# Zero products for an idle TensorE, and a longer reckoned way from a matmul to its reader, in a scheduled attention and GLU block

## The chip, the cores and the metric

The kernel runs on one core of one Trainium2 chip. The metric is device time in microseconds (us), lower is better. A run here is one execution; every comparison is made between runs of the changed program and runs of the kernel before on the same chip in the same rounds. Ratios are the mean time of one kernel's fast runs over that of the other's of the same rounds, so they are not quite the ratio of the medians that are quoted.

The engines: TensorE (PE; its weight loads are PEld), VectorE (DVE), ScalarE (ACT), GpSimd (POOL), SyncE (SP, which here only issues DMAs).

## The reference, cut to what matters

```python
x = A_x                                                   # 1 x 2048 x 640, bf16
h  = x + attention(layernorm(x), A_wqkv) @ A_wo           # 32 heads of 20
h2 = h + ((n @ w_gate) * (n @ w_up)) @ w_down             # n = layernorm(h), F = 1728
```

Attention has 32 heads x 2048 x 2048 scores. Their exponentials are the bulk of ACT's work; a part of them is made on DVE by a bit trick. The score products use 20 rows of the array, four heads side by side in four row groups; the products with the values fill 32 columns, four heads side by side in four column groups.

Of the kernel before, what the change touches and what calls it, by code (L numbers as in the profile page):

```python
# [17 lines left out]
P = 128  # L18
# [39 lines left out]


LAT = 0.12  # L60
DMA_LAT = 1.5
SWITCH = 0.105


def c_act(n):
# [78 lines left out]
def kernel(  # L144
# [30 lines left out]
    R = sb.tile([P, RW], BF16, name="R")  # L175
    WO = sb.tile([P, KT, D], BF16, name="WO")
    IDN = sb.tile([P, P], BF16, name="IDN")
    NEA, NEB, NY = 5, 4, 28
    EA = [sb.tile([P, 1536], BF16, name=f"EA{i}") for i in range(NEA)]
    EB = [sb.tile([P, 1024], BF16, name=f"EB{i}") for i in range(NEB)]  # L180
# [53 lines left out]
            heapq.heappush(coming[e], (op.avail, seq[0], op))  # L234
        tick(op.avail)

    def finish(op, t):
        op.done = t
        for u in op.users:
            u.left -= 1  # L240
            u.avail = max(u.avail, t)
            if u.left == 0:
                if isinstance(u, Op):
                    enqueue(u)
                else:
                    release_later(u.avail, u.cb)
        op.users = []
        tick(t)
# [31 lines left out]
    def try_start(e):  # L280
        t = now[0]
        if free[e] > t + 1e-9:
            return False
        c = coming[e]
        while c and c[0][0] <= t + 1e-9:
            _, s_, op = heapq.heappop(c)
            heapq.heappush(ready[e], (op.key, s_, op))
        held = []
        got = None
        while ready[e]:  # L290
            item = heapq.heappop(ready[e])
            op = item[2]
            if op.done is not None:
                continue
            if op.gate is not None and not op.gate():
                held.append(item)
                continue
            other = "POOL" if e == "DVE" else "DVE"
            if op.lock and e in lockt and lockt[other] > t + 1e-9:
                held.append(item)  # L300
                tick(lockt[other])
                continue
            got = op
            break
        for h_ in held:
            heapq.heappush(ready[e], h_)
        if got is None:
            return False
        end = t + (got.dur[e] if isinstance(got.dur, dict) else got.dur)
        free[e] = end  # L310
        if got.lock and e in lockt:
            lockt[e] = end
        if got.hook is not None:
            got.hook(t, end, e)
        got.fn(e)
        finish(got, end + got.lat)
        tick(end)
        return True

# [36 lines left out]
    with tc.manual_schedule():  # L356
# [3 lines left out]
            nc.gpsimd.memset(VX[:, :, hh * VS:hh * VS + 11], 1.0)  # L360
        nc.gpsimd.memset(VX[:, :, Dh:H * VS:VS], 1.0)
        nc.vector.memset(GSt[:], 0.0)
        free["DVE"] = 1.5
        free["POOL"] = 6.0
        free["SP"] = 0.75
# [112 lines left out]

        pe = {"free": 0.0, "mode": "D", "next": 0.0, "grp": [0.0] * 4, "end": 0.0}

        def pe_issue(mode, grp, dur):
            t = max(now[0], pe["next"])
            if mode != pe["mode"]:
                t = max(t, pe["end"] + SWITCH)
                pe["mode"] = mode
                pe["grp"] = [0.0] * 4
            if mode == "D":
                t = max(t, pe["end"])
            else:
                t = max(t, pe["grp"][grp])  # L490
            end = t + dur
            pe["next"] = t + 0.0035
            if mode != "D":
                pe["grp"][grp] = end
            pe["end"] = max(pe["end"], end)
            return t, end
# [455 lines left out]
        acs_n = [0]  # L952
        acs_use = [None, None]
        bc_use = [None]
        act_pend = [0]
        dve_units = [0]

        for ci in range(len(CHUNKS)):
# [57 lines left out]
        def refill(name, dbanks):  # L1016

            st = sets[name]
            st["state"] = "full"
            st["free_at"] = 1e9  # L1020
            used = set()
            ditems = []
            for i in dbanks:
                it = take_for_dve(used)
                if it is not None:
                    used.add(it[2])
                    ditems.append((i, it))
            items = []
            for i in range(st["n"]):
                it = take_next(used)  # L1030
                if it is not None:
                    used.add(it[2])
                    items.append(it)
            n = len(items)
            pairs = [(banks[name][i], items[i]) for i in range(n)] + [(banks["D"][i], it) for i, it in ditems]
            ends = rows_into(pairs)
            for q, (i, it) in enumerate(ditems):
                fill_d(i, it, ends[n + q])
            if not n:
                st["state"] = "free"  # L1040
                return
            end = max(ends[:n])
            src = (SA if name == "SA" else SBk)
            eslot = {}

            def hook(t, en, e):
                eslot["i"] = st["efree"].pop(0)
                left = [0]

                def rel():  # L1050
                    left[0] -= 1
                    if left[0] == 0:
                        st["efree"].append(eslot["i"])
                        tick(now[0])
                for i, it in enumerate(items):
                    left[0] += len(it[3])
                for i, it in enumerate(items):
                    queue_pieces(it, 3, [st["e"][eslot["i"]][:, i * 512:(i + 1) * 512]], en + LAT, rel)

                def fr():  # L1060
                    st["state"] = "free"
                    act_pend[0] -= 1
                release_later(en + LAT, fr)
                st["free_at"] = en + LAT

            def fn(e):
                nc.scalar.activation(st["e"][eslot["i"]][:, 0:n * 512], src[:, 0:n * 512], ACT.Exp, scale=SCALE)  # L1067
            z = Mark()
            z.done = end + LAT
            act_pend[0] += 1  # L1070
            add("ACT", c_act(512 * n), fn, (1,), [z], hook=hook, gate=lambda: bool(st["efree"]))

        def fill_d(i, it, end):
            bank = banks["D"][i]
            bank_use["D"][i] = "exp"
            z = Mark()
            z.done = end + LAT
            ys = [None] * 4
            dve_units[0] += 1

# [52 lines left out]
        def emit_piece(j):  # L1133
            ci, g = order_cg[cg_i[0]]
            cw = CHUNKS[ci][1]
            key = (ci, g, j)
            kt, ap, t, rel = pieces_q[key].popleft()
            n = emitted.get(key, 0)
            emitted[key] = n + 1
            last = acount.get(key, 0) == NT and n + 1 == expected[key]  # L1140
            h = 4 * g + j
            _, end = pe_issue("C", j, 0.216 * cw / 512)
            nc.tensor.matmul(ACC[32 * j:32 * j + 32, 0:cw], lhsT=VX[:, kt, h * VS:h * VS + 32], rhs=ap,  # L1143
                             start=(n == 0), stop=last, tile_position=(0, 32 * j), skip_group_check=True)
            release_later(end + LAT, rel)
            if last:
                acc_state["left"] -= 1
                if acc_state["left"] == 0:
                    acc_state["left"] = 4
                    close_group(ci, g, end)  # L1150
            return end
# [5 lines left out]
        def close_group(ci, g, end):  # L1157
            q0, cw = CHUNKS[ci]
            z = Mark()
            z.done = end + LAT  # L1160
            k = ngrp[0] % 2
            d = ngrp[0] % NDS
            ngrp[0] += 1
# [51 lines left out]
        def job_ready(jb):  # L1215
            if jb.can is not None and not jb.can():
                return False
            for d in jb.deps:
                if d.done is None or d.done > now[0] + 1e-9:
                    return False  # L1220
            return True
# [37 lines left out]
        def job_done(jb):  # L1259
            cur_job[0] = None  # L1260
            z = Mark()
            z.done = jb.end + LAT
            op = jb.evac(banks[jb.bank[0]][jb.bank[1]], z)
            bk = jb.bank

# [10 lines left out]
        def bg_step():  # L1276
# [8 lines left out]
            jb.i += 1  # L1285
            if step[0] == "T":
                _, c_, slot = step
                _, jb.end = pe_issue("D", 0, 0.064)
                nc.tensor.transpose(bank.bitcast(BF16)[:, c_ * P:(c_ + 1) * P], slot["t"][1][:, c_ * P:(c_ + 1) * P], IDN[:])
            else:  # L1290
                lhs, rhs, c0, c1, M, first, last, dur = step
                _, jb.end = pe_issue("D", 0, dur)
                nc.tensor.matmul(bank[0:M, c0:c1], lhsT=lhs(0, M), rhs=rhs(), start=first, stop=last,  # L1293
                                 skip_group_check=True)
            if jb.i == len(jb.mms):
# [96 lines left out]
        def pe_turn():  # L1392
# [5 lines left out]
            else:  # L1398
                r = to_refill()
                if r is not None:  # L1400
                    attn["started"] = True
                    refill(*r)
                    return pe_rest()
            n = 0
            over = attn["over"]
            while n < (1 if over else ROUNDS):
                if n and (urgent() or min(s_["free_at"] for s_ in sets.values()) < pe["end"] - 0.1):
                    break
                c = counts()
                if over and c is not None and sum(c) and c_round(c, False, False):  # L1410
# [7 lines left out]
                if not c_round(c, late and not short(), hold):  # L1418
                    break
                n += 1  # L1420
            return pe_rest() if n else False

        ROUNDS = 4
        WLO, WHI = 20, 50
# [27 lines left out]
        def to_refill():  # L1452
# [3 lines left out]
            if not names:  # L1456
                return None
            db = d_banks()
            if len(names) == 1 and not db and free["ACT"] - now[0] > THR and attn["started"]:
                tick(free["ACT"] - THR)  # L1460
                return None
            return names[0], db
# [76 lines left out]
```

## The kernel before: what the change and the argument touch

The builder of the program contains a planner. It simulates the engines with fixed costs, decides which instruction comes next on each engine, and emits them in that order. On the chip, each engine then runs the list that was emitted for it: e17 and e18 further down, 14 us apart at the end, run the same 718 ACT instructions in the same order.

```python
LAT = 0.12                       # from an instruction's end to its reader, us
SWITCH = 0.105
def c_act(n): return 0.10 + 0.833e-3 * n

def finish(op, t):               # t = end + LAT
    for u in op.users:
        u.avail = max(u.avail, t)
...
def pe_issue(mode, grp, dur):    # the planner's model of TensorE: D full, R row groups, C column groups
    t = max(now[0], pe["next"])
    if mode != pe["mode"]:
        t = max(t, pe["end"] + SWITCH)
    ...
def pe_turn():
    ... # a score set is free: refill it
    n = 0
    while n < (1 if over else ROUNDS):
        if n and (urgent() or min(s_["free_at"] for s_ in sets.values()) < pe["end"] - 0.1):
            break
        ... # one round of value products and background products
    return pe_rest() if n else False
```

A group of four heads ends with a chain through DRAM: DVE copies the accumulator (`acs<-ACC`), SP sends the denominators out and back (`dscr<-acs`, `dn<-dscr`), DVE takes reciprocals (`rn<-dn`), and they go out and come back broadcast.

The softmax here doesn't subtract the row's maximum and nothing guards it: scores larger than these inputs give would overflow.

## Time and profile before

869.8 us, median of 3 runs (869.73 to 870.98). The page's first part, busy us and share of the span for each engine, and from its second part the granted clock of TensorE in 40 slices (9 is 90% or more):

```profile
PE 806.7 (93%) x14491; PEld 388.5 (45%) x14491; DVE 734.2 (84%) x2002; ACT 757.3 (87%) x711; POOL 353.6 (41%) x520
PEclk9999999999999999999999999999899999999999
```

Three engines are nearly full. The groups of instructions that hold ACT's exponentials (busy us, mean ns of one, then the idle time of ACT just before them and what ended it):

```profile
L1067 ACT ACTIVATE EA<-SA 128x1536 bf16<-128x1536 f32 x316 | 460.3, 1457 | 24.3 <-PE SA L992 16.4 <-PE SB L992 4.4 <-PE D L992 0.4
L1067 ACT ACTIVATE EB<-SB 128x1024 bf16<-128x1024 f32 x315 | 324.3, 1030 | 20.4 <-PE SB L992 17.6 <-PE D L992 1.0 <-PE ACC L1143 0.2
```

ACT's 44.7 us of idle time end with score products: ACT waits for TensorE, not the reverse.

The clock hides more than the slices show. Busy time by stretches of 1 us, columns: stretch, length, busy us (instructions) of PE, PEld, DVE, ACT, POOL, then the granted clock, DMA share and GB/s:

```profile
417.00:418.00 1.00, 0.93 (x13) 0.29 (x7) 1.00 (x5) 1.00 (x2) 0.29 (x1) 1.00 0.19 41
418.00:419.00 1.00, 0.81 (x7) 0.31 (x5) 0.97 (x3) 1.00 (x2) 0.92 (x2) 1.00 0.55 166
419.00:420.00 1.00, 0.37 (x6) 0.16 (x5) 1.00 (x3) 1.00 (x2) 0.23 (x1) 1.00 0.39 135
420.00:421.00 1.00, 1.00 (x17) 0.41 (x16) 1.00 (x5) 1.00 (x2) 0.54 (x1) 0.74 0.05 10
421.00:422.00 1.00, 1.00 (x13) 0.17 (x4) 1.00 (x4) 0.88 (x1) 0.78 (x2) 0.50 0.03 8
422.00:423.00 1.00, 1.00 (x10) 0.21 (x6) 0.48 (x3) 0.07 (x1) 0.56 (x1) 0.50 0.07 7
```

TensorE is thinly used from 417 to 420 us, then its clock is halved for 3.4 us, DVE and ACT run dry at 422. There are six such dips before the end, each of 3.4 us. One dip leaves out 1.7 us of full clock (3.4 us at half). I call the sum of what is left out "missing clock"; here it is 10.2 us. TensorE was busy for 2.52 of the 3.41 us before the dip at 420.47 us, and its clock halved all the same.

The start, from the timeline of TensorE, and TensorE's instruction fetch in the first 25 us, from the DMA queues (packets, MB, share of 16 engines' span):

```profile
11.13 1.25 PE L1289 MATMUL D<-IDN,t 128*128 128x128 bf16 x10 [11.13 <-DVE t L453]
12.43 1.51 PE L1293 MATMUL D<-R 128*128 128x160 bf16 x10
```

```profile
q8 instruction: 1, 0.02, 0.3%
```

At the start TensorE idles for 11.1 us, then starts cold (ten transposes in 1.25 us; at 24.60 us five take 0.45). One block of instructions is fetched. Over the span this queue moves 113 blocks, and the page counts 28,982 matmuls and weight loads of TensorE: 256.5 to a block. So I take the queue to be TensorE's, and a block to be 256 instructions, an estimate from these counts.

### The profile page before, as it was taken

Reading aid. Unit: us, or ns where it says so; the run is one execution under the profiler, and the core shown is the slowest. Engines: PE = TensorE matmul, PEld = TensorE weight load, DVE = VectorE, ACT = ScalarE, POOL = GpSimd, SP = SyncE. Lnnn points to the kernel's source line nnn. Section 1 sums busy time; section 2 is a strip of 40 time slices with the busy share of each in tenths; the row PEclk is TensorE's granted clock in tenths of the full one; section 3 lists DMA queues with packets and bytes.
Section 4 is the critical chain, followed back from the end, with each engine's and each line's share of the span. In section 5 each row is a group of like instructions: output and inputs, shape, how many; then the busy total and the mean of one; then the engine's idle time right before and its main releaser. Section 6 shows DMA issues by size and latency. Waiting matters only on the chain.

```text
span 869.4 us, 34285 instructions
## 1 busy us (share of the span) xinstructions
PE 806.7 (93%) x14491; PEld 388.5 (45%) x14491; DVE 734.2 (84%) x2002; ACT 757.3 (87%) x711; POOL 353.6 (41%) x520
## 2 busy tenths in 40 slices
PE   4998999999988999999999999999899989999978
PEld 2432434333333444444233444443455555564856
DVE  6787899888899989998999998988899898896343
ACT  5787999999999999999999999999899999997211
POOL 1034444344454444444545444445445444443000
PEclk9999999999999999999999999999899999999999
DMA  9454321222135301011111011101011121003100
GB/s 272 63 163 126 96 72 39 93 69 76 54 108 132 100 25 50 26 44 33 32 29 31 22 25 45 45 23 37 22 34 41 40 32 35 20 13 53 30 16 16
DMA packets 70537, 49.64 MB, mean 57 GB/s; under 512 B 33712, under 2 KB 66448, under 8 KB 70384
## 3 DMA queue, kind: packets, MB, share of 16 engines
q1 hardware_dynamic: 70384, 47.46, 20.8%
q8 instruction: 113, 1.85, 0.9%
q14 instruction: 40, 0.33, 0.1%
HBM read 30.88 MB, written 10.32 MB: 47 GB/s over the span
## 4 chain that ended last, share of the span: by engine, by line
PE 57%; DVE 20%; DMA 9%; ACT 9%; issue 3%; SPq 1%; POOL 0%; DVEq 0%; ACTq 0%
PE D L1316 20%; PE ACC L1143 15%; DVE Y L1092 7%; PE D L1293 7%; PE SA L992 6%; DVE Y L1102 6%; ACT EA L1067 5%; PE D L992 4%; PE SB L992 4%; ACT EB L1067 4%; DMA dn<-dscr 3%; DMA dscr<-acs 2%; DMA qscr<-HH 1%; DVE acs L1172 1%; DVE HH L826 1%
## 5 line engine op out<-in xcount | busy, mean ns | idle before, releaser
L1067 ACT ACTIVATE EA<-SA 128x1536 bf16<-128x1536 f32 x319 | 462.1, 1449 | 24.3 <-PE SA L992 16.4
L1100 POOL TENSOR_SCALAR Y<-Y 128x512 uint16<-128x512 uint16 x467 | 305.9, 655 | 406.9 <-DVE Y L1102 270.1
L1092 DVE TENSOR_SCALAR Y<-D 128x512 uint16<-128x512 f32 x467 | 318.1, 684 | 54.0 <-PE SB L992 17.6
L1067 ACT ACTIVATE EB<-SB 128x1024 bf16<-128x1024 f32 x315 | 324.3, 1030 | 20.4 <-PE SB L992 17.6
L1143 PE MATMUL ACC<-Y,VX 128*32 128x512 bf16 (+1 forms) x2356 | 265.6, 343 | 4.9 <-DVE acs L1172 3.9
L1102 DVE TENSOR_SCALAR Y<-Y 128x512 uint16<-128x512 uint16 x934 | 252.0, 316 | 3.0
L1143 PE MATMUL ACC<-EA,VX 128*32 128x512 bf16 (+1 forms) x1186 | 215.7, 343 | 1.3 <-ACT EA L1067 1.1
L992 PE MATMUL D<-QT,KTt 20*128 20x512 bf16 (+1 forms) x589 | 177.7, 339 | 13.5 <-DVE Y L1092 8.9
L992 PEld LDWEIGHTS <-KTt 20*128 20x128 bf16 x2560 | 72.6, 91 | 220.9 <-issue 211.6
L1143 PE MATMUL ACC<-EB,VX 128*32 128x512 bf16 (+1 forms) x785 | 169.4, 343 | 0.3 <-ACT EB L1067 0.3
L1316 PEld LDWEIGHTS <-R 128*32 128x32 bf16 x5370 | 124.4, 96 | 95.6 <-issue 75.4
L1143 PEld LDWEIGHTS <-VX 128*32 128x32 bf16 x4327 | 119.6, 97 | 95.5 <-issue 72.8
L992 PE MATMUL SA<-QT,KTt 20*128 20x512 bf16 (+1 forms) x1186 | 130.4, 342 | 9.5 <-ACT EA L1067 8.1
L1316 PE MATMUL D<-L,R 128*32 128x256 bf16 x3240 | 129.4, 274 | 3.1 <-DMA L<-t 1.6
L992 PE MATMUL SB<-QT,KTt 20*128 20x512 bf16 (+1 forms) x785 | 126.1, 342 | 2.5 <-ACT EB L1067 2.1
L1316 PE MATMUL D<-R 128*32 128x160 bf16 (+1 forms) x2130 | 106.2, 301 | 5.5 <-DVE VX L325 3.0
L826 DVE TENSOR_TENSOR HH<-D,gs 128x256 bf16<-128x256 f32 x112 | 46.9, 419 | 21.9 <-ACT gs L323 21.1
L1201 POOL TENSOR_TENSOR os<-acs,bc 128x512 bf16<-128x512 f32 (+1 forms) x40 | 42.9, 1073 | 54.6 <-DMA bc<-rscr 20.9
L1316 PE MATMUL D<-R,HH 128*32 128x320 bf16 x1136 | 55.3, 301 | 1.8 <-DVE HH L826 1.6
L323 ACT CAST gs<-D 128x256 bf16<-128x256 f32 (+1 forms) x28 | 10.4, 372 | 33.1 <-PE D L1293 33.1
L1316 PEld LDWEIGHTS <-HH 128*32 128x32 bf16 x1136 | 27.1, 96 | 22.4 <-issue 17.5
L325 DVE CAST gs<-D 128x256 bf16<-128x256 f32 x84 | 34.7, 413 | 2.2 <-PE D L1316 1.3
(65 smaller groups left out, 356.6 us busy)
## 6 DMA issues: line engine op xcount, KB each, us to landing
bc<-rscr SPq DMA_DIRECT2D x24, 256.0 KB
KTt<-kscr SPq DMA_DIRECT2D x6, 512.0 KB
QT<-qscr SPq DMA_DIRECT2D x22, 128.0 KB
t<-in_A_x_dram SPq DMA_DIRECT2D x16, 160.0 KB
out_dram<-t SPq DMA_DIRECT2D x16, 160.0 KB
bc<-rscr SPq DMA_DIRECT2D x16, 128.0 KB
R<-in_B_w_gate_dram SPq DMA_DIRECT2D x4, 480.0 KB
R<-in_B_w_up_dram SPq DMA_DIRECT2D x4, 480.0 KB
```

What stands on the lines that cost most here:

```text
L323: nc.scalar.copy(o, i)
L325: nc.vector.tensor_copy(o, i)
L826: mu = add("DVE", c_psum(256), lambda e: nc.vector.tensor_tensor(HH[0:M, f, :], bank[0:M, 256:512], GS[k][0:M, :], ALU.mult), EVK, mdeps)
L992: nc.tensor.matmul(bank[:, n * cw:(n + 1) * cw], lhsT=KTt[32 * j:32 * j + Dh, g, kt * P:(kt + 1) * P], rhs=QTt[32 * j:32 * j + Dh, g, 0:cw ...
L1067: nc.scalar.activation(st["e"][eslot["i"]][:, 0:n * 512], src[:, 0:n * 512], ACT.Exp, scale=SCALE)
L1092: p_ = add("DVE", c_psum(512), lambda e: nc.vector.tensor_scalar(YT[ys[0]][:, :], bank, scalar1=EXP_A, scalar2=EXP_B, op0=ALU.mult, op1=AL ...
L1100: nc.gpsimd.tensor_scalar(o, i_, scalar1=float(d), scalar2=1.0, op0=ALU.add, op1=ALU.mult)
L1102: nc.vector.tensor_scalar(o, i_, scalar1=float(d), scalar2=None, op0=ALU.add)
L1143: nc.tensor.matmul(ACC[32 * j:32 * j + 32, 0:cw], lhsT=VX[:, kt, h * VS:h * VS + 32], rhs=ap, start=(n == 0), stop=last, tile_position=(0, ...
L1201: mu = add("POOL", 0.1 + 2.3e-3 * cw, lambda e: nc.gpsimd.tensor_tensor(o[:, 0:cw], a[:, 0:cw], BC[0][:, 0:cw], ALU.mult), (0,), d4 + os_u ...
L1293: nc.tensor.matmul(bank[0:M, c0:c1], lhsT=lhs(0, M), rhs=rhs(), start=first, stop=last, skip_group_check=True)
L1316: nc.tensor.matmul(bank[32 * j:32 * j + 32, c0:c1], lhsT=lhs(32 * j, 32 * j + 32), rhs=rhs(), start=first, stop=last, tile_position=(0, 32 ...
```

## The change

Its intent: (1) where TensorE would idle and was too little used over the last 3.413 us (a constant of the planner, as long as the dips measured above), the planner emits products of an all-zero 128x32 weight with the identity, four side by side, into the accumulator bank, adding zero; (2) the planner reckons 0.23 us instead of 0.12 from a matmul to its reader; (3) none at all between chained work of one engine; (4) it stops background rounds 0.2 us earlier before a score set comes free.

```diff
+LATP = 0.23
+WINDOW = 3.413
+    ZW = sb.tile([P, 32], BF16, name="ZW")
-    def finish(op, t):
+    def finish(op, t, e=None, end=None):
-            u.avail = max(u.avail, t)
+            u.avail = max(u.avail, end if e is not None and isinstance(u, Op) and u.engs == (e,) and e != "SP" else t)
+        nc.vector.memset(ZW[:], 0.0)
+        def recent(t):            # share of the array used in the last WINDOW, from a list that pe_issue keeps
-            z.done = end + LAT    # 5 places: after scores, value products, background products
+            z.done = end + LATP
-            return pe_rest() if n else False
+            if rounds():
+                return pe_rest()
+            return keep_busy()
+        BUSY = 0.55
+        def keep_busy():
+            t = now[0]
+            if t < T0 or ...:                                   # T0 = 4.0
+                return False
+            if recent(t) > (BUSY if attn["started"] else BUSY0):   # BUSY0 = 0.7
+                tick(t + 0.25)
+                return False
+            rhs = bass.AP(tensor=IDN.tensor, offset=IDN.offset, ap=[IDN.ap[0], [0, NB], [1, P]])   # NB = 1
+            ...                                                 # to = ACC, or a free bank while ACC is copied out
+            for j in range(4):
+                pe_issue("C", j, 0.054 * NB)
+                nc.tensor.matmul(to[32 * j:32 * j + 32, 0:P * NB]..., lhsT=ZW[:], rhs=rhs, start=...,
+                                 stop=False, tile_position=(0, 32 * j), skip_group_check=True)
+            pe["free"] = pe["end"] - 0.03
+            tick(pe["free"])
+            return True
-                if n and (urgent() or min(s_["free_at"] for s_ in sets.values()) < pe["end"] - 0.1):
+                if n and (urgent() or min(s_["free_at"] for s_ in sets.values()) < pe["end"] + AHEAD):   # 0.1
```

The order of instructions: 1,276 zero products, of them 348 before the first transpose. 445 instead of 467 score tiles go to DVE.

## The prediction

> **What bounds the kernel now.** Three engines are close to full together: on the page's first part PE 93%, ACT 87%, DVE 84% of 869.4 us. The stretches from 130 to 783 us have ACT and PE at about 96%. ACT does two exponentials, 128x1536 and 128x1024, every 2.23 us (starts 415.92, 418.15, 420.39 in the timeline). The groups of instructions give 24.3 + 20.4 = 44.7 us of idle ACT before these, nearly all released by score matmuls. From 801 us to the end the chain of waits is nearly all full-array products (196 in 24.1 us, 0.123 us each).
>
> **The clock.** The stretches cut to 1 us show six places with the granted clock at 0.50, each for 3.4 us: 79-83, 420-424, 611-615, 622-626, 799-803, 840-843. In all 10.2 us of full clock are missing. Each follows about 3 us in which PE waited (419-420: busy 0.37, while the accumulator was being copied out; 796-797: busy 0). [...] Matmuls stretch from 0.38 to 0.61 us; ACT then waits 1.05 us at 422.9. PE also starts cold: five transposes take 0.73 us at 11.1, 0.40 us at 24.7.
>
> **What the change adds.** From the instruction order, 1,276 zero products of 128 columns, four side by side, so 319 sets. A warm set is estimated at 54 ns, a quarter of the 0.22 us that a set of 512 columns takes: 17 us in all. 87 sets stand before the first transpose, where PE waits for data; 39 in the tail, nearly all where it waits for the last layer norm; 193 sets (10 us) lie in some 40 runs between the first and the last score, where the plan has PE idle. The order is fixed, so a run costs time where PE is late.
>
> **What it moves.** 445 instead of 467 score tiles go to DVE, 1,603 instead of 1,581 to ACT. ACT gets 22 x 0.446 = 10 us more; DVE loses 22 x (0.60 + 2 x 0.21) = 22 us; PE loses 66 value products, 3.6 us. PE stops background work earlier before a score set frees, which should shorten ACT's waits. After the last score 140 instead of 168 full-array down products remain: 28 x 0.136 = 3.8 us less.
>
> **Sum.** Dips avoided: at most 10.2 us, I take 6, since real idle places are not quite the planned ones. Tail -3 to -4 us. Warm start -1 us. Shift to ACT: +10 us of work, of which the shorter waits give back some 8. Zero products where PE is late: +2 us. Together about -8 us: **861 us, 8 in 10 between 846 and 873**. Faster by over 2%: 0.2; within 2%: 0.76; slower: 0.04.
>
> **What would show it.** Clock: mean over 0.988, at most two dips left, none between last layer norm and the end. First transposes near 0.4 us. ACT: idle before exponentials below 38 us although its busy time grows by about 10. DVE busy some 20 us lower. The part after the last exponential shorter by 5 us.
>
> **What would make it wrong.** The dips might not be on the critical path, or zero products might not count as activity; then only the tail is left, about 866. If ACT idles as before, its added 10 us show fully: 870 or more. If ACT's waits nearly vanish, 845.

What is left for the clock is what the trace before showed: six dips, each after a stretch in which TensorE waited (in the idlest us of the four before each, in order of time, it was busy for 0.00, 0.37, 0.48, 0.27, 0.00 and 0.00). The five transposes at 24.7 us begin at 24.60 in the timeline and take 0.45 us.

## The result, and the profile after

881.94 us, median of 4 runs (881.72 to 882.63), against 870.39 us before; ratio 1.0133, 95% interval 1.0115 to 1.015. By the 2% rule the class is "same", but it is clearly slower, and above the range of the prediction. The page and the exponentials:

```profile
PE 820.1 (93%) x15755; PEld 412.6 (47%) x15755; DVE 724.5 (82%) x1938; ACT 770.5 (88%) x718; POOL 333.8 (38%) x498
PEclk8999999999999999999999999999999999999999
```

```profile
L1083 ACT ACTIVATE EA<-SA 128x1536 bf16<-128x1536 f32 x320 | 465.3, 1454 | 19.0 <-PE SA L1008 13.9 <-PE SB L1008 1.7 <-PE D L1008 0.3
L1083 ACT ACTIVATE EB<-SB 128x1024 bf16<-128x1024 f32 x319 | 327.8, 1028 | 21.6 <-PE SB L1008 13.4 <-PE D L1008 5.6
```

After the start only two dips are left (711 and 765 us): the zero products do keep the clock up. One execution doesn't settle the number, though: the second profile of the same program (e5) has five dips after the start, and ACT waits 43.9 us in it. Here ACT waits 40.6 us, a little less than before, and has 13 us more to do. The start is what nobody asked for. From the timelines of TensorE and ACT, and the DMA queues of the first 25 us:

```profile
1.36 4.85 PE L1447 MATMUL ACC<-IDN,ZW 128*32 128x128 bf16 x223 [1.36 <-POOL IDN masks.py:199]
9.53 1.95 PE L1447 MATMUL ACC<-IDN,ZW 128*32 128x128 bf16 x125 [3.31 <-issue]
11.41 0.34 PE L1307 MATMUL D<-IDN,t 128*128 128x128 bf16 x3
15.72 0.91 PE L1307 MATMUL D<-IDN,t 128*128 128x128 bf16 x7 [3.98 <-issue]
```

```profile
24.86 1.45 ACT L1083 ACTIVATE EA<-SA 128x1536 bf16<-128x1536 f32 x1 [0.18 <-PE SA L1008]
```

```profile
q8 instruction: 3, 0.05, 0.9%
```

The zero products wait for nothing once the identity is made, so they do not fill the gap: they run from 1.4 us on, the first 223 in 4.85 us. TensorE then stands still twice, 3.3 and 4.0 us, with nothing that the profile can name ("issue"), the second time in the middle of a row of transposes whose data lie ready. Between the two stops it did 125 zero products and 3 transposes: with a weight load for each, 256 instructions, one block. Fetches begin at 6.5, 13.0 and 19.25 us, and TensorE goes on at 9.53 and 15.72. The clock falls to half while it stands (3.4 us of missing clock at 14 to 21 us), and the first exponential starts at 24.86 us instead of 19.65.

In the tail, the last copy of the accumulator starts 65.7 us before the end in the kernel before (803.70 of 869.4) and 61.8 us in this one: 4 us gained, as predicted. But 1.7 of the 4 us are a dip (840 us) that this execution does not have after its last copy. e5, the same program with such a dip there, has 63.4 us, so the shorter tail itself gains some 2.3. At the third such copy (111.5 us in both) the two kernels are level, since the one before loses more time there to other waits; they part after that: 3.7 us at the tenth, 7.3 at the twentieth, 14.4 at the last.

### The profile page after: what moved, and what is told of

The parts are those of the page before. It is cut to its first block, busy times and chain, and to the rows that moved or that the text cites. A ratio compares the mean times of both kernels' runs of the same rounds, so it can differ in the third digit from the quotient of the medians.

```text
span 879.9 us, 36714 instructions
## 1 busy us (share of the span) xinstructions
PE 820.1 (93%) x15755; PEld 412.6 (47%) x15755; DVE 724.5 (82%) x1938; ACT 770.5 (88%) x718; POOL 333.8 (38%) x498
## 4 chain that ended last, share of the span: by engine, by line
PE 46%; DVE 23%; DMA 12%; ACT 9%; issue 5%; SPq 3%; POOL 1%; DVEq 0%; POOLq 0%; ACTq 0%
PE D L1334 16%; PE ACC L1159 11%; DVE Y L1108 7%; DVE Y L1118 5%; DMA dn<-dscr 5%; PE D L1311 5%; PE SA L1008 5%; ACT EA L1083 5%; PE SB L1008 4%; ACT EB L1083 4%; PE D L1008 2%; DMA dscr<-acs 2%; SPq L1221 2%; DVE HH L842 2%; DMA L<-t 2%
## 5 line engine op out<-in xcount | busy, mean ns | idle before, releaser
L1083 ACT ACTIVATE EA<-SA 128x1536 bf16<-128x1536 f32 x323 | 468.0, 1449 | 19.1 <-PE SA L1008 13.9
L1116 POOL TENSOR_SCALAR Y<-Y 128x512 uint16<-128x512 uint16 x445 | 285.8, 642 | 444.7 <-DVE Y L1118 303.3
L1108 DVE TENSOR_SCALAR Y<-D 128x512 uint16<-128x512 f32 x445 | 303.5, 685 | 57.4 <-PE SA L1008 20.0
L1118 DVE TENSOR_SCALAR Y<-Y 128x512 uint16<-128x512 uint16 x890 | 238.3, 311 | 8.7
L1159 PE MATMUL ACC<-EA,VX 128*32 128x512 bf16 (+1 forms) x1203 | 209.1, 341 | 1.3 <-ACT EA L1083 0.9
L1159 PE MATMUL ACC<-EB,VX 128*32 128x512 bf16 (+1 forms) x796 | 177.8, 340 | 0.0
L1008 PE MATMUL D<-QT,KTt 20*128 20x512 bf16 (+1 forms) x561 | 168.6, 337 | 8.9 <-DVE Y L1108 5.8
L1334 PE MATMUL D<-L,R 128*32 128x256 bf16 x3240 | 137.1, 275 | 11.3 <-DVE HH L842 7.7
L1334 PE MATMUL D<-R,HH 128*32 128x320 bf16 x1236 | 64.6, 306 | 4.7 <-DVE HH L842 4.2
L842 DVE TENSOR_TENSOR HH<-D,gs 128x256 bf16<-128x256 f32 x104 | 44.0, 423 | 17.0 <-ACT gs L327 14.3
L1334 PEld LDWEIGHTS <-HH 128*32 128x32 bf16 x1236 | 33.7, 97 | 25.8 <-issue 20.6
L1334 PE MATMUL D<-WO,ON 128*32 128x320 bf16 x560 | 31.7, 304 | 4.6 <-DVE hr L766 2.4
```

Source lines behind the costliest of these rows:

```text
L842: mu = add("DVE", c_psum(256), lambda e: nc.vector.tensor_tensor(HH[0:M, f, :], bank[0:M, 256:512], GS[k][0:M, :], ALU.mult), EVK, mdeps)
L1008: nc.tensor.matmul(bank[:, n * cw:(n + 1) * cw], lhsT=KTt[32 * j:32 * j + Dh, g, kt * P:(kt + 1) * P], rhs=QTt[32 * j:32 * j + Dh, g, 0:cw ...
L1083: nc.scalar.activation(st["e"][eslot["i"]][:, 0:n * 512], src[:, 0:n * 512], ACT.Exp, scale=SCALE)
L1108: p_ = add("DVE", c_psum(512), lambda e: nc.vector.tensor_scalar(YT[ys[0]][:, :], bank, scalar1=EXP_A, scalar2=EXP_B, op0=ALU.mult, op1=AL ...
L1116: nc.gpsimd.tensor_scalar(o, i_, scalar1=float(d), scalar2=1.0, op0=ALU.add, op1=ALU.mult)
L1118: nc.vector.tensor_scalar(o, i_, scalar1=float(d), scalar2=None, op0=ALU.add)
```

## The experiments

Two aids for reading them. First, executions of one program differ in their dips: the kernel before took 863.54 us at a mean clock of 0.992 and 875.87 at 0.978 on one chip. A fit through all 132 runs with a clock on record, of 19 programs (one constant for each program, one common slope; an estimate) gives 0.75 us of time for each us of missing clock, with a standard error of 0.04 and a scatter of 1.6 us. "At full clock" below is a program's constant in this fit, with a standard error of 0.7 to 1.5 us; for the changed kernel the 3.4 us that its cold start leaves out are not counted as missing, so that they stay in its constant. This was not done for the four other programs whose clock record is at half around the first transposes (in the profiled runs 3.4 us in e4 and e9, 1.7 in e6 and e8). Treated alike they would stand at 864.1 (e4), 868.0 (e9), 869.2 (e6) and 860.4 (e8). The programs without early zero products are cold there too (ten transposes in 1.25 us), but their clock records begin only at the first rise, so that nothing is counted as missing. Second, nothing was changed but what the diff says: `EMIT` is the zero product's `nc.tensor.matmul` in `keep_busy`, and where only it is made conditional, plan and order of all other instructions stay those of the changed kernel.

| run | what | ratio to before (95%) | mean us | missing us | at full clock |
|---|---|---|---|---|---|
| before | (44 runs on all chips) | 1 | 872.0 | 14.3 | 861.3 |
| e5 | the change, again | 1.0137 (1.0076 to 1.0197) | 883.3 with its first runs | 12.1 | 876.7 |
| e1 | no zeros at the start | 0.9947 (0.9881 to 1.0012) | 867.2 | 4.1 | 864.1 |
| e2 | no zeros at all, same order | 1.0064 (1.0002 to 1.0125) | 877.3 | 20.1 | 862.3 |
| e3 | new planner, planned without zeros | 1.0109 (1.0035 to 1.0182) | 881.3 | 30.6 | 858.4 |
| e4 | old planner with zeros | 0.9998 (0.9923 to 1.0073) | 870.9 | 12.6 | 861.5 |
| e6 | start: 88 products, 512 wide | 1.0029 (0.9965 to 1.0093) | 875.1 | 9.6 | 867.9 |
| e7 | start: 348 products, 32 wide | 1.0132 (1.0061 to 1.0203) | 884.1 | 11.9 | 875.1 |
| e8 | e4, start 92 products, 512 wide | 0.9943 (0.9876 to 1.001) | 867.6 | 11.3 | 859.1 |
| e9 | start: 128 products (256 instructions) | 1.0001 (0.997 to 1.0031) | 872.1 | 9.0 | 865.4 |
| e10 | e1, chained latency back | 1.0081 (1.0038 to 1.0124) | 879.1 | 8.5 | 872.8 |
| e11 | old planner with zeros, none at the start | 0.9906 (0.9869 to 0.9943) | 864.0 | 5.6 | 859.8 |
| e12 | e1, 0.12 us to the reader | 1.0059 (1.0023 to 1.0096) | 877.2 | 10.2 | 869.6 |
| e13, e14 | e11, 0.5 ns more, less per exponential | 0.9933, 0.9979 | 866.4, 870.4 | 6.9, 8.3 | 861.3, 864.2 |
| e15, e16 | e1, 0.5 ns more, less per exponential | 1.001, 0.9998 | 873.1, 872.1 | 7.8, 5.2 | 867.2, 868.1 |
| e17 | start: 384 products, 32 wide (768 instructions) | 0.999 (0.9961 to 1.0018) | 870.9 | 6.4 | 866.1 |
| e18 | start: 92 products, 32 wide (184 instructions) | 1.011 (1.0066 to 1.0153) | 881.5 | 10.3 | 873.8 |

All gave correct results.

### First batch: which part costs the time

```diff
 e1  -EMIT   + if attn["started"]: EMIT
 e2  -EMIT   (keep_busy and the plan unchanged)
 e3  -            return keep_busy()
     +            return False
 e4  -LATP = 0.23                       +LATP = 0.12
     -... end if e is not None ... else t     +u.avail = max(u.avail, t)
     -AHEAD = 0.1                       +AHEAD = -0.1        (gate on far-off jobs removed)
```

Planned without zero products, the planner of e4 gives TensorE the same list, matmul for matmul, as the kernel before (built and compared). With them it plans a different order: 463 instead of 467 tiles on DVE.

> The changed kernel with its plan and order kept, but the 348 zero products before the first transpose are not emitted. Theory 1 (the zero products at the start use up the fetched instructions, and TensorE then waits 3.3 and 4.0 us for more while the input loads fill the DMA engines): the two waits at 6 and 12 us vanish, first exponential near 19.7 us instead of 24.9. How much of that 5 us reaches the end: all of it would give 877 us; none, because the waits for the query and key rows at 60 to 110 us swallow it, 881 to 882. Rival (zero products at the start are harmless, the loss lies elsewhere): first exponential still past 23 us.

> The changed kernel with its plan and order kept, but no zero product emitted at all. If the zero products themselves cost the time (array time and instructions): 870 us or less. If the new order (1,603 tiles on ACT, readers planned later) costs it: 876 to 882, about as much as with the start's alone off, plus or minus what the clock dips that come back take (each about 1.7 us; I expect 3 to 6 dips).

> The changed planner (0.23 us from a matmul to its reader, 0.1 us margin for background rounds, chained work on one engine without latency) with the zero products taken out of plan and program: 456 tiles on DVE. Theory 2 (the plan costs the time): 875 to 882 us. Rival (the zero products cost it): 868 to 872.

> The old planner with zero products added (1,124 of them, 463 tiles on DVE). Theory 2: 868 to 874 us, that is about the kernel before, with the start's 5 us lost or swallowed and some dips gone. Rival (the zero products cost it): 878 to 884.

e1: both stops are gone, the first exponential is at 19.85 us, and the time is below anything I expected: 0.9947 of before instead of 1.0133. The 348 zero products at the start cost about 16 us (0.019 of 872), three times the delay of the first exponential. So the start is the cause of the loss, but its 5 us are not the whole of it. With it gone, ACT's waits are those that the prediction hoped for, 34.1 us:

```profile
L1083 ACT ACTIVATE EA<-SA 128x1536 bf16<-128x1536 f32 x320 | 465.4, 1454 | 20.2 <-PE SA L1008 14.3 <-PE SB L1008 1.7 <-PE D L1008 0.9
L1083 ACT ACTIVATE EB<-SB 128x1024 bf16<-128x1024 f32 x319 | 327.6, 1027 | 13.9 <-PE SB L1008 10.9 <-PE D L1008 0.8
```

That e1 is faster than the kernel before is not shown: the interval of its ratio includes 1.

e2 against e1 tells what the other zero products are worth in this order: without them 877.3 us and 20.1 us of missing clock, with them 867.2 and 4.1. They gain 10 us, by the fit all of it through the clock; at full clock they cost about 2. One rival was not tested: leaving out 928 products also moves all later instructions along the fetched blocks, and the fifth batch shows that this alone can cost as much (10 us). Products of all-zero weights did keep the clock up here: 4.1 us of missing clock with them, 20.1 without. e3: the new planner alone is slower than before, at 1.0109, but by the fit not at full clock: it idles TensorE so that 30.6 us of clock are missing. Theory 2, "the plan costs the time", is right about the sum and wrong about how. e4: the rival that zero products as such cost the time is refuted. Its first exponential is late as well, at 23.9 us.

The same can be seen as an account of TensorE. From 20 us to the end, I added up its gaps of over 0.25 us in its timeline, and the missing clock of the dips in that stretch, and took the remainder as work:

| program (profiled run) | gaps | missing clock | remainder |
|---|---|---|---|
| before | 39.1 | 10.2 | 800.1 |
| e2, no zeros | 41.2 | 22.2 | 793.9 |
| e1, zeros, none at the start | 29.2 | 6.8 | 812.2 |
| e11, old planner, zeros, none at the start | 25.2 | 6.8 | 810.9 |

From e2 to e1, gaps shrink by 12.0 us and missing clock by 15.4, and work grows by 18.3. From before to e11, whose orders differ, the three are 13.9, 3.4 and 10.8. The zero products turn gaps into work, and the gain comes in the first pair from the clock alone, in the second from gaps and clock. That TensorE is the scarce engine here, and its missing clock costs time for that reason, fits the slope of 0.75 but was not tested by itself.

### Second batch: what the start costs

```diff
 e6  -EMIT  + if attn["started"] or zn[0] % 4 == 1: EMIT with 4 x 128 columns at the start   (zn counts the calls)
 e7  -rhs = ... [1, P]]      + rhs = ... [1, P if attn["started"] else 32]]
 e8  e4 with the edit of e6
```

> The changed kernel itself once more, so that it shares a chip and rounds with the next three. 1.01 to 1.015 of the kernel before; the two waits of TensorE at 6 and 12 us as in its first profile. If the clock records explain the spread between runs (in the first batch the kernel before took 863.5 us at a mean clock of 0.992 and 875.9 at 0.978, near one us for each us of full clock missing), its runs order themselves by clock too.

> The changed kernel, same plan and order, but the 348 zero products of 128 columns at the start are 88 of 512 columns: the same array time, a quarter of the instructions. Fetch theory: no wait of TensorE that nothing releases before the transposes, first exponential before 20.5 us, time within 4 us of the run with the start's zero products off (0.995 of before). Rival (the array time or the power of the zero products at the start costs it): as the changed kernel, 1.01 or more.

> The changed kernel, same plan and order, the 348 zero products at the start 32 columns wide instead of 128: a quarter of the array time, the same number of instructions. Fetch theory: two waits of 3 to 5 us that nothing releases remain (the first may begin earlier), first exponential past 23 us, time as the changed kernel, 1.01 or more. Rival (array time): as with the start's off, 0.995.

> The old planner with zero products, those at the start 512 columns wide (92 instead of 368 matmuls). In the first batch the old planner with all zero products took 1.000 of before with a first exponential at 23.9 us. Fetch theory: first exponential before 20.5 us and 3 to 8 us faster, 0.99 to 0.997 of before, perhaps below both kernels. Rival: 1.000 as before.

e6: the same array time in a quarter of the instructions. No stop, transposes at 11.31 us (ten in 0.81 us, so the warm start comes), and 9 us less than the change. e7: a quarter of the array time in as many instructions. The start of TensorE in e6, then in e7:

```profile
1.37 7.34 PE L1452 MATMUL ACC<-IDN,ZW 128*32 128x512 bf16 x88 [1.37 <-POOL IDN masks.py:199]
11.31 0.81 PE L1307 MATMUL D<-IDN,t 128*128 128x128 bf16 x10 [2.60 <-DVE t L458]
```

```profile
1.37 2.02 PE L1448 MATMUL ACC<-IDN,ZW 128*32 128x32 bf16 x223 [1.37 <-POOL IDN masks.py:199]
7.14 1.20 PE L1448 MATMUL ACC<-IDN,ZW 128*32 128x32 bf16 x125 [3.75 <-issue]
```

The first stop is there, 3.8 us after 223 zero products, as in the change; no second one comes before the transposes, which start at 11.25 us. With a quarter of the instructions in the same array time there is no stop, with a quarter of the array time in the same instructions there is: by these two runs it is instructions that TensorE runs out of, not time on the array. The second stop of the change, after exactly 256 more, fits the size of a block taken from the counts above, and so does that of e17, after 128 zero products with their weight loads (the first came after 447 recorded instructions in the change, and why there stays open). In the change TensorE stood still 3.3 and 4.0 us, and went on about 3 us after a fetch had begun (6.5 and 13.0 us), under the input loads (307 GB/s from 6 to 16 us, against a mean of 57). e8 has no stop either (first exponential at 19.69 us) and takes 0.9943 of before where e4 takes 0.9998, which is within what I expected.

But e7 fell in its main point: I expected a late first exponential and the time of the change from it. It had the time of the change (1.0132) without the delay. So delay at the start could not be the whole cause. Something else came with those instructions.

### Third batch: how many instructions, and which part of the planner

```diff
 e9   + if attn["started"] or zn[0] <= 32: EMIT
 e10  e1 with   +u.avail = max(u.avail, t)       (latency in chains of one engine, as before)
 e11  e4 with the edit of e1
 e12  e1 with   +LATP = 0.12
```

> The changed kernel, same plan and order, with only the first 128 of the 348 zero products at the start: with their weight loads 256 instructions, one fetched block, so that every later instruction lies as in the run with the start's zero products off, one block further on. Fetch theory: no wait that nothing releases before or in the first transposes, first exponential before 20.5 us, time within 3 us of the run with the start's zero products off at the same clock (that run: 867 us at a mean clock of 0.995). Rival (any zero products at the start cost, about 3 us for each hundred): 870 to 872 at that clock.

> The run with the start's zero products off, and the planner again adds 0.12 us between chained work of one engine (the change had dropped it). If dropping it is what makes TensorE come too early for the gated products: idle of TensorE that ends with the product HH on VectorE falls from 8 us (12 in the changed kernel) to 2 to 4 us (2.2 in the kernel before), and the time at the same clock by 3 to 6 us. Rival: these waits stay and the time is within 2 us.

> The old planner with zero products in the middle and the tail only, none emitted at the start. The same with all of them had a first exponential at 23.9 us and 1.000 of before. Fetch theory: first exponential near 20 us, 0.985 to 0.995 of before; at full clock 857 to 859 us by the line through all runs. Rival (start does not matter with the old planner): 1.000.

> The run with the start's zero products off, with 0.12 instead of 0.23 us from a matmul to its reader: 463 tiles on DVE instead of 445, 716 zero products. If the longer way costs time (18 tiles more on ACT, more waiting planned): 3 to 8 us faster at the same clock. If it pays (fewer DVE tiles need 54 value products less on TensorE, which is the scarce engine): 2 to 5 us slower at the same clock. Clock theory: mean clock at or above 0.99.

e9: 128 zero products at the start cause no stop and cost little (865.4 at full clock against 864.1, or 868.0 with the cold start kept in), and gain nothing, since TensorE is cold again when the data come (ten transposes in 1.25 us). e10: the wait of TensorE for the gated products fell nearly as I said, from 9.1 to 4.8 us, but it is 9 us slower at full clock, the opposite of my theory. In the profiled runs the loss lies in the tail: from the last copy of the accumulator to the end e10 takes 73.8 us, e1 63.4. e12: slower by 5.5 us at full clock. Two parts of the planner's change were undone alone (the earlier stop of background rounds was not), and each is worse than both all of it and none of it, so the parts do not add up. e11, the old planner with zero products in the middle and tail but none at the start, beats both kernels: 0.9906 of before, 863.89 us median of 6 runs against 872.97. Its page, its exponentials and the clock:

```profile
PE 814.8 (94%) x15243; PEld 403.3 (47%) x15243; DVE 727.1 (84%) x1990; ACT 759.5 (88%) x714; POOL 350.5 (41%) x516
PEclk9998999999999999999999999999999999999999
```

```profile
L1083 ACT ACTIVATE EA<-SA 128x1536 bf16<-128x1536 f32 x316 | 460.5, 1457 | 23.3 <-PE SA L1008 17.9 <-PE SB L1008 2.9 <-PE D L1008 0.2
L1083 ACT ACTIVATE EB<-SB 128x1024 bf16<-128x1024 f32 x317 | 326.9, 1031 | 11.9 <-PE SB L1008 8.4 <-PE D L1008 1.6
```

ACT's waits are 35.2 us, 9.5 less than before.

### Fourth batch: is it the planner, or any re-planning?

```diff
 e13, e15  -return 0.10 + 0.833e-3 * n    +return 0.1005 + 0.833e-3 * n     (in c_act; on e11, on e1)
 e14, e16                                 +return 0.0995 + 0.833e-3 * n
```

> Old planner, zero products in the middle and tail, with 0.5 ns more reckoned for each exponential. Scatter theory: up to 8 us away from the run without this (864 us, 0.991 of before), either way. If the planner is stable: within 2 us at the same clock.

> The same with 0.5 ns less. Scatter theory: up to 8 us away from 864, either way. If stable: within 2 us at the same clock.

> New planner, zero products in the middle and tail, none at the start, 0.5 ns more reckoned for each exponential (453 tiles on DVE instead of 445). Scatter theory: anywhere from 862 to 880 at the same clock, overlapping the old planner's two. If the new planner is worse in itself: both its runs slower than both of the old one's by 4 us or more.

> The same with 0.5 ns less (446 tiles on DVE). Scatter theory: 862 to 880 at the same clock. If the new planner is worse in itself: slower than both runs of the old planner by 4 us or more.

A constant without meaning moves the time at full clock by up to 4.4 us (e11, 859.8; e13, 861.3; e14, 864.2) and 4.0 us (e1, 864.1; e15, 867.2; e16, 868.1). The three of the new planner average 866.5 us, the three of the old one 861.8, but the best of them equals the worst of the old one's. That the new planner is worse in itself is likely, not shown; a single part's effect of a few us, as in e10 and e12, is of the size of this scatter or not far above it.

### Fifth batch: the shift against the blocks

What else do instructions at the start do? They push all later ones along the blocks of 256 instructions that I took from the counts. The change and e7 have 696 more there than e1, which is two blocks and 184. So e17 adds three whole blocks and e18 only the 184.

```diff
 e17  e7, and the first 9 of 87 sets emitted twice     (384 products)
 e18  e7 with  + if attn["started"] or zn[0] <= 23: EMIT     (92 products)
```

> 384 zero products of 32 columns at the start: 768 instructions, three whole blocks, so nothing later shifts against the block boundaries. If the shift costs the 10 us: 863 to 867 us at full clock by the line through all runs. If the number of instructions at the start costs it: 872 to 877.

> 92 zero products of 32 columns at the start: 184 instructions, the same shift against the block boundaries as 348, and no shortage at the start (no wait that nothing releases). If the shift costs: 872 to 877 us at full clock. If the number costs: 863 to 867.

Of these two theories the shift is right and the number is not. 384 products in whole blocks are almost free (866.1 at full clock); 92 products, with no stop at the start at all, cost 10 us (873.8). e1, e9 and e17, whose later instructions lie alike in their blocks, are within 2 us of each other at full clock (within 4 with e9's cold start kept in); e7 and e18, shifted by 184, within 1.3.

But a shift has no fixed price. e6 has 88 products at the start, a shift of 176, nearly that of e18, and stands at 867.9 (869.2 with its cold start kept in), though its first transposes ran warm. e8 has 92, exactly the shift of e18, in the old planner's order, and stands at 859.1 (860.4), level with e11, which has none (859.8). So the 10 us belong to this shift in this order. That what a shift does elsewhere depends on which transfers the fetches then meet is a guess that no run tests.

How a fetch may cost time is seen at one place. SP's timeline in e17, then in e18 (start, us, what; in each a line `QT<-qscr` before the last is left out):

```profile
153.31 0.72 SPq L357 DMA_DIRECT2D qscr<-L  x1
154.21 0.79 SPq L357 DMA_DIRECT2D KTt<-kscr  x2
155.10 0.56 SPq L357 DMA_DIRECT2D dscr<-acs  x1
159.37 0.32 SPq L357 DMA_DIRECT2D dn<-dscr  x1
```

```profile
153.47 0.72 SPq L357 DMA_DIRECT2D qscr<-L  x1
154.47 2.00 SPq L357 DMA_DIRECT2D KTt<-kscr  x2
156.56 0.56 SPq L357 DMA_DIRECT2D dscr<-acs  x1
160.46 0.32 SPq L357 DMA_DIRECT2D dn<-dscr  x1
```

The two programs are level up to the first line. Then SP needs 2.00 us for the same two DMA issues that took 0.79, and all that SP does later is late. In e17 a block of TensorE's instructions was fetched at 152.0 us, in e18 at 154.50 (fetches are given by the quarter of a us in which they begin). What waits for the denominators, from the timelines of DVE and TensorE, e17 first:

```profile
161.56 0.25 DVE L1192 RECIPROCAL rn<-dn 128x16 f32<-128x16 f32 x1 [0.56 <-DMA dn<-dscr]
162.05 0.53 PE L1334 MATMUL D<-R 128*32 128x160 bf16 x20 [1.01 <-DVE VX L329]
```

```profile
163.13 0.25 DVE L1192 RECIPROCAL rn<-dn 128x16 f32<-128x16 f32 x1 [1.97 <-DMA dn<-dscr]
163.62 0.86 PE L1334 MATMUL D<-R 128*32 128x160 bf16 x20 [2.41 <-DVE VX L329]
```

DVE stands 1.97 us before the reciprocal instead of 0.56, TensorE stands 2.41 us behind DVE instead of 1.01, and here its clock then drops (20 products in 0.86 us instead of 0.53; 3.4 us of missing clock, what two dips leave out). A fetch beside two issues has, it seems, become 1.4 us of waiting and these 3.4 us. The second step is not certain: the kernel before has the long issue (2.11 us) and no dip after it, and e8 has the dip (166 to 173 us) without the long issue. This place in nine programs' profiles (two of them are of the change):

| program | SP at `KTt<-kscr`, us | issue takes, us | nearest fetches, us |
|---|---|---|---|
| e17 | 154.21 | 0.79 | 152.0, 159.25 |
| e9 | 153.89 | 0.79 | 151.75, 158.75 |
| e1 | 153.30 | 0.79 | 150.5, 158.25 |
| e6 | 152.84 | 0.79 | 156.0 |
| e18 | 154.47 | 2.00 | 154.50 |
| e7 | 155.96 | 1.49 | 156.0 |
| the change, again | 157.56 | 1.24 | 157.0 |
| the change | 157.43 | 1.80 | 157.25 |
| before | 158.53 | 2.11 | 158.75 |

Five of five with a fetch within 0.6 us take 1.24 us or more, four of four without one take 0.79. Of the other eleven profiles, e14 and e16 have a fetch 0.3 and 0.1 us after and take 1.92 and 1.65 us; e3 has one 0.5 us before and takes 0.82, the one exception; the other eight have none within 0.6 us and take 0.79 to 0.87. The same holds over the whole of all twenty profiles after 100 us. Of 1,639 SP issues with such a fetch under way in their first 0.4 us, 195 took over 0.3 us longer than is usual (the median) for their transfer; of 6,736 with none within 0.3 us, 13 did. So a fetch goes with a long issue, though most issues beside one are not long. That it lengthens them is the reading that fits; how it would do so inside the DMA system, no run shows.

How much of the 10 us is this? The excess of such long issues adds up to 10.8 us in e18, 11.1 in the change and 9.1 in e7, against 4.5 in e17, 5.3 in e1, 7.4 in e9 and 4.9 in e6. But the kernel before has 7.9 and is fast, so the sum alone does not set the time. I followed only this place to its end. e17 and e18 run the same 718 ACT instructions in the same order, so that e18's lag can be read off them (at e17's times): 0.2 us at 154 us, 3.6 at 172, 4.3 at 265, 5.8 at 273, 7.8 at 687, 12.1 at 731, 14.0 at the end. This place accounts for 3.4 of the 14 us. That the same collision makes the other steps is argued, not shown.

## Why the prediction was wrong, point by point

- **The step that failed: "Warm start -1 us", and with it "87 sets stand before the first transpose, where PE waits for data".** I took them as free, since TensorE idles there, and costed only their array time. The runs showed instead that these products cost some 16 us (e5 against e1, ratios 1.0137 and 0.9947). By the constants at full clock (876.7 and 864.1) it is 12.6 us: 9.7 come with the shift of 184 instructions, which caused no stop in e18; that the other 3 or so come from the stops and the cold start that they bring is inferred, and hardly above the fit's error; the rest of the 16 is clock that those runs happened to lack. Array time has no part in it (e7). That the shift acts through fetches beside SP's DMA issues is shown at one place and argued for the rest.
- **"Dips avoided: 6 us".** Right in kind and size. In the change, dips after the start fall from six to two in the profiled run (five in e5); over all runs the clock missing after the start falls from 14.3 to 8.7 us. The zero products are worth 10 us in the new order (e2 to e1) and, with the re-planning that they bring, 8 us with the old planner (before to e11, 0.9906), mostly through the clock. My upper bound of one us for each us of missing clock is close to the fitted 0.75.
- **"Tail -3 to -4 us".** The 4.0 us measured look right, but 1.7 of them are a dip that the profiled run lacks, already counted above. By e5, with that dip, the tail is 2.3 us shorter: right in kind, a little too large.
- **"Shift to ACT: +10 us, of which shorter waits give back some 8".** ACT's busy time grew by 13 us and its waits shrank by 4 in the change, so the 38 us that I named as a sign were missed (40.6). In the same order without the start (e1) the waits shrank by 10.6, to 34.1, against 12.4 us more of work: there this term is +2, as predicted. The products at the start, and what followed from them, took that gain away again. What the planner's part costs in all is about 5 us at full clock (three plans against three), inside the scatter of re-planning, and its single parts cannot be told apart.
- **"Zero products where PE is late: +2 us".** It fits: e1 and e2 differ by 2 us at full clock, with an error of 1.4 and the shifted blocks as a rival.
- **"DVE busy some 20 us lower".** It is 9.7 us lower (734.2 to 724.5); the count of tiles was right, but the page counts time in which instructions overlap once; their durations added up fall by 31 us (867.1 to 835.9). It did not matter, as DVE was not the engine that bounds.
- **"First transposes near 0.4 us".** The first three took 0.34 us, and then came the stop of 4 us, which nothing in my argument allowed for.

Without the products at the start the change takes 867 us on this evidence (e1), inside the range.

## What to carry to other kernels

Filler instructions were not free where TensorE idled: they waited for nothing, so they ran early (from 1.4 us on); TensorE then stood still for 3.3 and 4.0 us; and they moved every later instruction along the fetched blocks, which cost 10 us in one order and nothing in another. So make them few and wide (88 instead of 348 at the start took 9 us less at full clock), or leave out those before the data arrive (some 16 us less). In this kernel filling TensorE's gaps paid through its clock (8 to 10 us of 870) although it did no useful work. And before a reordering is judged by a few us, measure the scatter of orders that differ by nothing that matters.
